# Re-ordering a retention-plus-routing kernel: when a batch's ranks, gathers, stores and transposes are issued

## The chip, the cores and the metric

The kernel runs on one core of one Trainium2 chip. The metric is device time in microseconds (us), the median of several runs. The core has a matrix engine (PE, whose weight loads the profile lists apart as PEld), a vector engine (DVE), a scalar engine (ACT), GpSimd (POOL) and a sync engine (SP). In this kernel SP issues all loads of inputs and weights, and POOL issues all stores, gathers and scatters, so each engine's instructions and DMA issues run in the order in which the program lists them.

## The reference

There are 8 batches of 576 rows with 8 heads of 64 columns, so a row is 512 wide. First comes a causal attention without softmax, whose scores decay with distance; then only the 128 rows of each batch with the highest gate score go through a two-layer MLP and are added back.

```python
scores = q @ k.T / sqrt(64)                      # per batch and head
gamma  = 1 - 2.0 ** (-5 - arange(H))
Dmat   = where(rel >= 0, gamma ** rel, 0)
x      = (scores * Dmat) @ v                     # (B, S, 512) after joining the heads
# for each batch b, capacity = 128
s      = x[b] @ w_gate
top    = argpartition(-s, capacity)[:capacity]
h      = maximum(x[b, top] @ w1, 0)              # 512 -> 1024
out[b]      = x[b]
out[b, top] = x[b, top] + sigmoid(s[top])[:, None] * (h @ w2)
```

## The kernel before

**Tiles and steps.** A batch is cut into 9 chunks of 64 rows, which makes 72 chunks in all. A step handles two neighbouring chunks (both in one 128-partition tile), so there are 36 steps (`NS`), and the loop of lines 489 to 517 runs over them, with a 37th pass that finishes the last one. A batch has an odd number of chunks, so every second batch ends in the middle of a step. `ends[b]` is the first step after batch b's last chunk has been started: 5, 9, 14, 18, 23, 27, 32, 36.

**One step.** SP loads four 256 KB pieces of a later step (q, k, v, and k again in another layout) into one of 8 `raw` buffers (lines 103 to 107). `scaled` (line 142) multiplies v by decays into `vs`, on POOL, or on ACT for the three steps that `by_act` names. `block(s)` (line 207) issues the step's matmuls on PE with 64x64 operands: the scores (`sc_ps`), the state updates (`u_ps`, copied to `st` by ACT), and, in between, the product of the step before (`crosswise(s - 1)`, into `y_ps`). `masked` (line 230, DVE) applies the causal mask and gives `am`, which the next step's `crosswise` reads. `values` (line 236, DVE) rescales `y_ps` into `xs`, the finished rows, and reduces each half with the gate weights to a score per row (`sc`). `store` (line 254, POOL) writes the rows to the output of their batch in DRAM.

**Choosing 128 rows of a batch.** When all nine chunks have scores, `total` (line 273, two small matmuls and two ACT copies) adds the two head halves, `spread` (line 288, PE and an ACT copy) lays the 576 scores out along every partition (`row`), and `compare` (line 303, DVE) counts for 128 rows at a time how many rows are ahead of each: a rank. There are five such groups, four `full` ones and one of 64 rows. Where counts are made in two parts, `joined` adds them. `one_hot` (line 318, DVE) turns ranks into a selection matrix, `rows` (line 326, PE and an ACT cast) turns that into row numbers (`idx`), and `gather` (line 337, POOL, an indirect DMA) reads those rows of the output tensor back from DRAM into `xr`. As it reads the batch's output tensor, it waits for the landing of the stores to that tensor.

**The MLP.** `turn` (line 352) transposes `xr` on PE (four transposes) and ACT copies the result to `xg`. `gates` (line 343) makes the gate. `mlp` (line 385) queues eight parts: four `up` (16 matmuls and an ACT ReLU each) and four `down` (4 matmuls each). The last `down` multiplies by the gate, adds the row and scatters the result from POOL. `some(n)` (line 389) takes n parts from that queue; `share` (lines 470 to 478) says how many a step takes.

**Order.** All of it is listed by hand. In an ordinary step the order is: loads, `run(before)`, `scaled(s + 1)`, `block(s)`, `masked(s)`, `run(mid)`, `values(s - 1)`, `store(s - 1)`, perhaps `scaled` on ACT, `run(early)`, `some(share)`, `run(late)`. `plan` puts a batch's work into one of those four slots of a step. For batches 1 to 6: total late in step `ends[b]`; spread early and three compares late in the next; the other compares and the one-hot mid, `rows` and `gather` late in `ends[b] + 2`; `turn` and `mlp` early, `gates` late in `ends[b] + 4`. Batch 0 has its own order in steps 4 and 5 (`first` and `second`, lines 413 to 440): all scores of chunks 0 to 7 are spread at once, `masked(5)` comes ahead of the last compares, and both halves of step 4's rows are stored at the end of `second`. Its `rows` and `gather` follow mid in step 6, its `turn` early in step 7.

**Loads.** `bring` (line 91) issues a load. With `few` it first waits for an earlier load so that about four are in flight; without, only the reuse of its eight semaphores limits it.

Of the kernel before, what the change touches and what calls it, by code (L numbers as in the profile page):

```python
# [9 lines left out]
F32 = mybir.dt.float32  # L10
# [25 lines left out]
def kernel(  # L36
# [66 lines left out]
    def load(s):  # L103
        x = loads.tile([P, 4, DM], F32, name="raw")
        for a in range(4):
            bring(x[:, a, :], qkvk[s, :, a * DM : (a + 1) * DM], few=s <= ends[0])
        raw[s] = x
# [31 lines left out]

    by_act = lambda s: ends[0] <= s < ends[0] + 3  # L140

# [111 lines left out]

    def store(s):
        (b, c), (b2, _) = batch(2 * s), batch(2 * s + 1)
        for i, half in enumerate(halves):
            x = xs[s][half, :].rearrange("p (c d) -> p c d", c=2)
            if b == b2:
                nc.gpsimd.dma_start(  # L259
                    out=outs[b][C * c : C * c + 2 * C, W * i : W * i + W]  # L260
                    .rearrange("(c p) d -> p c d", c=2), in_=x)
            else:
                nc.gpsimd.dma_start(out=outs[b][C * c : C * c + C, W * i : W * i + W],
                                    in_=x[:, 0, :])
                nc.gpsimd.dma_start(out=outs[b2][:C, W * i : W * i + W], in_=x[:, 1, :])

# [36 lines left out]
    def compare(b, k, j0=0, j1=S, part=0):  # L303
        if b not in rank:
            rank[b] = work.tile([P, 2, NK], F32, name="rank", bufs=2)
        n = size(k)
# [6 lines left out]

    def joined(b, n):
        nc.vector.tensor_tensor(out=rank[b][:, 0, :n], in0=rank[b][:, 0, :n],
                                in1=rank[b][:, 1, :n], op=OP.add)

# [91 lines left out]
    def go(fs):  # L409
        for f in fs:  # L410
            f()

    def first():

# [65 lines left out]
    AHEAD = 8  # L480
    bring(table, consts)
    constants()
    for s in range(AHEAD):
        load(s)
# [4 lines left out]
    for s in range(NS + 1):  # L489
# [13 lines left out]
        else:  # L503
# [4 lines left out]
            if s:  # L508
                values(s - 1)
                store(s - 1)  # L510
        if s == 2:
# [4 lines left out]
        some(share.get(s, 0))  # L516
        run(late, s)
    some(1)
    total(last, NC - 2, NC)
# [76 lines left out]
```

## Time and profile before

| | |
|---|---|
| median of 3 runs | 274.92 us (274.78 to 280.85) |
| the profiled execution | 274.87 us |
| its span in the trace | 273.2 us |
| PE busy | 231.0 us, 85% of the span |
| DVE busy | 141.7 us, 52% |
| POOL busy | 103.3 us, 38% |
| ACT busy | 58.7 us, 22% |
| moved by DMA | 56.83 MB |
| granted PE clock, mean | 0.933 |

The span is the trace's own length; the execution's time is 1.7 us longer. Busy time alone says little here: PE is the busiest engine, but the stretches in which it stands still differ along the span, so the profile is read by stage. The page's strip cuts the span into 40 slices of 6.8 us; the other views used are the waits per engine, the timeline of one engine in a stretch, and sums over stretches chosen by hand.

### The profile page before, as it was taken

How to read it: one execution, taken by the hardware profiler on the slowest of the kernel's cores; microseconds unless marked ns; L12 is line 12 of the kernel's file. 1: busy time of each engine (PE TensorE's matmuls, PEld its weight loads, DVE VectorE, ACT ScalarE, POOL GpSimd, SP SyncE). 2: the span in 40 equal slices, each digit the busy share in tenths (PEclk: the TensorE clock that was granted, in tenths of full speed). 3: DMA queues.
4: the chain of work that ended last, by engine and by line, in shares of the span. 5: the costliest groups of instructions: out<-in, count | busy, mean ns of one | idle time of the engine just before them, and what ended most of it. 6: DMA issues, size and time to landing. Idle time of an engine off the chain costs nothing.

```text
span 273.2 us, 11548 instructions
## 1 busy us (share of the span) xinstructions
PE 231.0 (85%) x5184; PEld 183.9 (67%) x5184; DVE 141.7 (52%) x354; ACT 58.7 (22%) x182; POOL 103.3 (38%) x138
## 2 busy tenths in 40 slices
PE   1845886089977999969999999699999998999992
PEld 1734785079753897649866986469868975894950
DVE  0333585243593538865864378818736487750101
ACT  1111164032210232113211231112212321121100
POOL 4264202804407353364163741824165525201101
PEclk9998568569998999999999999979999999999998
DMA  6879999999996786586577766866042113211000
GB/s 209 276 244 304 315 409 377 376 406 385 326 390 198 245 280 213 190 277 247 170 229 250 256 218 207 266 221 216 26 114 80 42 43 78 70 49 38 38 2 38
DMA packets 27601, 56.83 MB, mean 208 GB/s; under 512 B 4000, under 2 KB 4128, under 8 KB 27552
## 3 DMA queue, kind: packets, MB, share of 16 engines
q1 hardware_dynamic: 22688, 42.46, 46.6%
q0 software_dynamic: 4864, 13.64, 15.2%
q8 instruction: 41, 0.67, 1.0%
q14 instruction: 8, 0.07, 0.1%
HBM read 44.54 MB, written 11.53 MB: 205 GB/s over the span
## 4 chain that ended last, share of the span: by engine, by line
PE 60%; issue 14%; DMA 13%; DVE 8%; ACT 1%; POOLq 1%; POOL 1%; SPq 0%; DVEq 0%; ACTq 0%
PE h_ps L365 17%; PE ye_ps L373 11%; PE u_ps L165 9%; PE sc_ps L175 9%; DMA xr<-out,idx 7%; DVE scr L309 5%; DMA raw<-in_qkvk 5%; PE row_ps L296 5%; PE y_ps L196 4%; PE y_ps L186 3%; PE xg_ps L356 2%; DVE hot L322 1%; DVE am L232 1%; DMA out<-xs 1%; PE idx_ps L330 1%
## 5 line engine op out<-in xcount | busy, mean ns | idle before, releaser
L259 POOL DMA_DIRECT2D out<-xs x64 | 39.8, 625 | 90.3 <-DVE xs L241 89.9
L232 DVE TENSOR_TENSOR am<-sc_ps,table 128x512 f32<-128x512 f32 x36 | 24.9, 690 | 74.2 <-PE sc_ps L175 53.6
L365 PEld LDWEIGHTS h_ps<-xg,w_sb 128*128 128x128 f32 x512 | 59.5, 192 | 5.5 <-issue 4.4
L373 PE MATMUL ye_ps<-w_sb,hT 128*128 128x512 f32 x128 | 63.0, 624 | 0.0
L365 PE MATMUL h_ps<-xg,w_sb 128*128 128x128 f32 x512 | 62.2, 278 | 0.5 <-issue 0.4
L175 PE MATMUL sc_ps<-raw 64*64 64x64 f32 x1152 | 44.9, 231 | 11.0 <-DMA raw<-in_qkvk 5.9
L175 PEld LDWEIGHTS sc_ps<-raw 64*64 64x64 f32 x1152 | 41.0, 146 | 13.1 <-issue 7.0
L165 PE MATMUL u_ps<-vs,raw 64*64 64x64 f32 x1024 | 45.7, 232 | 3.3 <-ACT st L205 2.4
L186 PE MATMUL y_ps<-vs,am 64*64 64x64 f32 x1152 | 45.9, 232 | 3.0 <-issue 2.7
L309 DVE SCALAR_TENSOR_TENSOR scr<-row,rs,ahead 128x576 f32<-128x576 f32 (+5 forms) x47 | 42.7, 909 | 10.2 <-ACT row L301 6.1
L165 PEld LDWEIGHTS u_ps<-vs,raw 64*64 64x64 f32 x1024 | 38.1, 144 | 11.7 <-issue 6.4
L186 PEld LDWEIGHTS y_ps<-vs,am 64*64 64x64 f32 x1152 | 40.1, 144 | 3.6 <-issue 3.0
L205 ACT COPY st<-u_ps 128x256 f32<-128x256 f32 x64 | 23.7, 371 | 82.3 <-PE u_ps L165 60.9
L196 PE MATMUL y_ps<-st,raw 64*64 64x64 f32 x1024 | 39.7, 227 | 2.0 <-issue 2.0
L151 POOL TENSOR_TENSOR vs<-raw,table 128x512 f32<-128x512 f32 x33 | 34.7, 1052 | 13.3 <-DMA raw<-in_qkvk 12.8
L196 PEld LDWEIGHTS y_ps<-st,raw 64*64 64x64 f32 x1024 | 36.0, 143 | 2.1 <-issue 2.1
L373 PEld LDWEIGHTS ye_ps<-w_sb,hT 128*128 128x128 f32 x128 | 22.8, 195 | 19.5 <-issue 18.7
L250 DVE SCALAR_TENSOR_TENSOR scr<-xs,table 128x256 f32<-128x256 f32 x72 | 34.0, 473 | 2.5
L241 DVE TENSOR_TENSOR xs<-y_ps,table 128x512 f32<-128x512 f32 (+1 forms) x37 | 24.7, 667 | 3.9 <-PE y_ps L196 3.6
L367 ACT ACTIVATE hT<-h_ps 128x256 f32<-128x256 f32 x32 | 12.3, 383 | 55.7 <-PE h_ps L365 55.7
L378 DVE SCALAR_TENSOR_TENSOR o<-ye_ps,gate,xr 128x512 f32<-128x512 f32 x8 | 6.0, 751 | 30.3 <-PE ye_ps L373 17.5
L379 POOL DMA_INDIRECT out<-o,idx x8 | 9.5, 1187 | 31.1 <-DVE o L378 31.1
(35 smaller groups left out, 113.0 us busy)
## 6 DMA issues: line engine op xcount, KB each, us to landing
raw<-in_qkvk SPq DMA_DIRECT2D x144, 256.0 KB, 5.2
out<-xs POOLq DMA_DIRECT2D x64, 128.0 KB, 4.9
w_sb<-in_w SPq DMA_DIRECT2D x8, 512.0 KB, 8.9
out<-xs POOLq DMA_DIRECT2D x16, 64.0 KB, 4.9
wg<-in_w_gate SPq DMA_DIRECT2D x1, 256.0 KB
table<-in_consts SPq DMA_DIRECT2D x1, 234.5 KB
xr<-out,idx POOLq DMA_INDIRECT x8, 4.0
out<-o,idx POOLq DMA_INDIRECT x8, 4.1
```

What stands on the lines that cost most here:

```text
L151: nc.gpsimd.tensor_tensor(out=blocks(vs[s]), in0=blocks(raw[s][:, 2, :]), in1=dec[:, 0, HH * c : HH * c + H].unsqueeze(2).to_broadcast([P, ...
L165: yield lambda h=h, half=half: nc.tensor.matmul(u_ps[b][half, where(0, h)], raw[s][half, 3, where(e, h)], vs[s][half, where(e, h)], start= ...
L175: yield lambda e=e, h=h, half=half: nc.tensor.matmul(sc_ps[s][half, where(e, h)], raw[s][half, 1, where(e, h)], raw[s][half, 0, where(e, h ...
L186: yield lambda e=e, h=h, i=i, half=half: nc.tensor.matmul(y_ps[s][halves[1 - i], where(e, h)], am[s][half, where(e, h)], vs[s][half, where ...
L196: yield lambda g=g, e=e, h=h, i=i, half=half: nc.tensor.matmul(y_ps[s][halves[1 - i], where(e, h)], raw[s][half, 0, where(e, h)], st[g - 1 ...
L232: nc.vector.tensor_tensor(out=blocks(am[s]), in0=blocks(sc_ps[s]), in1=causal.unsqueeze(1).to_broadcast([P, H, C]), op=OP.mult)
L241: nc.vector.tensor_tensor(out=blocks(xs[s])[:, i0:i1, :], in0=blocks(y_ps[s])[:, i0:i1, :], in1=dec[:, 1, HH * c + i0 : HH * c + i1].unsqu ...
L250: nc.vector.scalar_tensor_tensor(scr, xs[s][:, W * e : W * e + W], 1.0, wgh, op0=OP.mult, op1=OP.mult, accum_out=sc[b][:, c : c + 1])
L259: nc.gpsimd.dma_start(out=outs[b][C * c : C * c + 2 * C, W * i : W * i + W] .rearrange("(c p) d -> p c d", c=2), in_=x)
L309: nc.vector.scalar_tensor_tensor(scr[:n, : j1 - j0], row[b][:n, j0:j1], rs[b][:n, k : k + 1], ahead[:n, at + j0 : at + j1], op0=OP.subtrac ...
L365: nc.tensor.matmul(t[:, a, :], w1_sb[:, d, P * (f + a) : P * (f + a) + P], xg[b][:, d, :], start=d == 0, stop=d == KD - 1)
L373: nc.tensor.matmul(ye[b], hT[b][:, a, :], w2_sb[:, a, :], start=a == 0, stop=a == FB - 1)
```

## The change

Six edits, all of order or of transfers:

1. `first` stores step 4's batch-0 half (the batch's last 64 rows) right after it is computed; the other half is stored in `second`.
2. Batch 0's ranks are made in three parts: columns of chunks 0 to 5 at the end of step 3, chunks 6 and 7 and then chunk 8 in steps 4 and 5. `rank` has a third slot and `joined` is called twice.
3. In `second` the compares, the one-hot, `rows` and `gather` come ahead of `masked(5)` and of the rest of the values and stores. `rows` and `gather` thus move from step 6 to step 5; the `turn` of batch 0 stays early in step 7.
4. In ordinary steps `store(s - 1)` moves to the very end of the step, behind `run(late)`, and so behind gathers and scatters on POOL.
5. For batches 1 to 6, `turn` and `mlp` move from early to late in the same step, and the parts are shared evenly from the next step on.
6. Step 5's loads are no longer `few`, its `vs` is made by POOL in place of ACT, and one small sigmoid is issued at the start.

```diff
-            bring(x[:, a, :], qkvk[s, :, a * DM : (a + 1) * DM], few=s <= ends[0])
+            bring(x[:, a, :], qkvk[s, :, a * DM : (a + 1) * DM], few=s < ends[0])
...
-    by_act = lambda s: ends[0] <= s < ends[0] + 3
+    by_act = lambda s: ends[0] < s < ends[0] + 3
...
-    def store(s):
+    def store(s, es=(0, 1)):
...
+            if 0 in es:
                 nc.gpsimd.dma_start(out=outs[b][C * c : C * c + C, W * i : W * i + W],
                                     in_=x[:, 0, :])
+            if 1 in es:
                 nc.gpsimd.dma_start(out=outs[b2][:C, W * i : W * i + W], in_=x[:, 1, :])
...
+    def part(b, k0, k1, c0, c1):
+
+        total(b, c0, c1)
+        spread(b, columns(k0, k1))
+
+    def ranked(b, k0, k1, part):
+        j0, j1 = P * k0, min(P * k1, S)
+        for k in range(k0):
+            compare(b, k, j0, j1, part)
+        for k in range(k0, k1):
+            compare(b, k, 0, j1)
...
         values(s - 1)
         store(s - 1)
-        total(0, 0, NC - 1)
-        spread(0, columns(0, full))
+        part(0, full - 1, full, 2 * full - 2, 2 * full)
         values(s, (0,))
-        total(0, NC - 1, NC)
-        spread(0, columns(full, NK))
+        store(s, (0,))
+        part(0, full, NK, 2 * full, NC)
         go(crosswise(s, (1,)))
-        for k in range(full):
-            compare(0, k, 0, P * full)
+        ranked(0, full - 1, full, 1)
 
     def second():
         s = ends[0]
         block(s, False)
+        ranked(0, full, NK, 2)
+        joined(0, full - 1)
+        joined(0, full, 2)
+        one_hot(0)
+        rows(0)
+        gather(0)
         masked(s)
-        for k in range(full):
-            compare(0, k, P * full, S, 1)
-        compare(0, full)
-        joined(0, full)
-        one_hot(0)
         values(s - 1, (1,))
-        store(s - 1)
-
-    s = ends[0] + 1
-    plan(mid, s, rows, 0)
-    plan(mid, s, gather, 0)
-    plan(early, s + 1, turn, 0)
-    plan(late, s + 1, mlp, 0)
-    plan(late, s + 1, gates, 0)
-    start = [s + 2]
+        store(s - 1, (1,))
+
+    s = ends[0]
+    plan(late, s - 2, part, 0, 0, full - 1, 0, 2 * full - 2)
+    plan(late, s - 2, ranked, 0, 0, full - 1, 0)
+    plan(early, s + 2, turn, 0)
+    plan(late, s + 2, mlp, 0)
+    plan(late, s + 2, gates, 0)
+    start = [s + 3]
...
-        plan(early, s + 4, turn, b)
-        plan(early, s + 4, mlp, b)
+        plan(late, s + 4, turn, b)
+        plan(late, s + 4, mlp, b)
         plan(late, s + 4, gates, b)
-        start.append(s + 4)
+        start.append(s + 5)
...
     share = {}
-    for i, (s0, s1) in enumerate(zip(start, start[1:])):
-        n = 0
-        for s in range(s0, s1 + 1):
-            most = 1 if s == s1 or (i and s == s0) else 2
-            more = min(most, 8 - n - (s1 - s))
-            share[s] = share.get(s, 0) + more
-            n += more
-        assert n == 8
+    for s0, s1 in zip(start, start[1:]):
+        n = s1 - s0
+        for i in range(n):
+            share[s0 + i] = -(-8 * (i + 1) // n) + (-8 * i // n)
...
     constants()
+    warm = work.tile([P, 1], F32, name="warm", bufs=1)
+    nc.scalar.activation(out=warm, in_=ones[:, :1], func=AF.Sigmoid)
...
             if s:
                 values(s - 1)
-                store(s - 1)
...
         run(late, s)
+        if s and s not in (ends[0] - 1, ends[0]):
+            store(s - 1)
```

More of the change, by code (lines that the diff above doesn't have):

```diff
@@ L261, in store @@
                     .rearrange("(c p) d -> p c d", c=2), in_=x)
-            else:
+                continue
+            if 0 in es:
                 nc.gpsimd.dma_start(out=outs[b][C * c : C * c + C, W * i : W * i + W],
                                     in_=x[:, 0, :])
+            if 1 in es:
                 nc.gpsimd.dma_start(out=outs[b2][:C, W * i : W * i + W], in_=x[:, 1, :])
@@ L304, in compare @@
         if b not in rank:
-            rank[b] = work.tile([P, 2, NK], F32, name="rank", bufs=2)
+            rank[b] = work.tile([P, 3, NK], F32, name="rank", bufs=2)
         n = size(k)
@@ L312, in compare, with joined @@
             op0=OP.subtract, op1=OP.is_gt, accum_out=rank[b][:n, part, k : k + 1])
-    def joined(b, n):
+    def joined(b, n, part=1):
         nc.vector.tensor_tensor(out=rank[b][:, 0, :n], in0=rank[b][:, 0, :n],
-                                in1=rank[b][:, 1, :n], op=OP.add)
+                                in1=rank[b][:, part, :n], op=OP.add)
     def one_hot(b):
```

## The prediction, made before the changed kernel was run

> **What bounds the kernel now.** I read the strip of 40 slices first, for where PE stands still, then PE's waits, then the timelines of the engines there, then the clock.
>
> ```profile
> PE   1845886089977999969999999699999998999992
> ...
> PEclk9998568569998999999999999979999999999998
> DMA  6879999999996786586577766866042113211000
> ```
>
> Before slice 8 (54 us) PE has holes, one of them a whole slice (7); after it PE is nearly full. So PE sets the end, and a hole taken away moves everything behind it. DMA is full from slice 4 to slice 11: loads could be late next. PE's waits:
>
> ```profile
> PE xg_ps L356 <- DMA xr<-out,idx: 12.6, 4, 7.5
> PE sc_ps L175 <- DMA raw<-in_qkvk: 5.9, 1, 5.9
> PE sc_ps L175 <- issue: 5.1, 3, 2.9
> PE idx_ps L330 <- DVE hot L322: 3.2, 4, 1.4
> ...
> PE y_ps L196 <- issue: 2.0, 1, 2.0
> ```
>
> Transposes waiting for gathers cost most: 12.6 us in four places. In PE's timeline they stand at 55.63 us (7.48, batch 0), 121.13 (2.23, batch 2), 177.84 (2.58, batch 4) and 251.52 (0.32, batch 7). Why the first is long, POOL's timeline tells:
>
> ```profile
> 30.98 0.53 POOL L263 DMA_DIRECT2D out<-xs  x1 [0.42 <-DVE xs L241]
> 42.19 0.53 POOL L265 DMA_DIRECT2D out<-xs  x1 [10.68 <-DVE xs L241]
> 42.71 0.52 POOL L263 DMA_DIRECT2D out<-xs  x1
> 43.22 0.52 POOL L265 DMA_DIRECT2D out<-xs  x1
> 48.73 1.03 POOL L339 DMA_INDIRECT xr<-out,idx  x1 [4.99 <-ACT st L205]
> ```
>
> Of batch 0's last rows one half is issued at 30.98 (L263), the other only at 42.71, because the store between them, of batch 1's rows, waits for DVE. The row numbers are ready at 42.46 (ACT's cast, 42.29 + 0.17), but the gather starts at 48.73: the L263 store of 42.71 takes 5.1 us to land, and the queue's own semaphore wait of the gather is 4.67 us. The releaser named (ACT st) isn't the one. The gather takes 6.9 us to land.
>
> **Edit by edit** (against 274.87 us, the profiled execution: 273.2 span and 1.7 around it; the median is 274.92, so the same sum serves).
>
> *Edits 1 to 3, batch 0.* Rank chain: before, row sums are spread by 34.72 us (ACT's second row copy, 34.51 + 0.21), four 512-wide compares (0.79 each) end at 36.94, `masked(5)` takes DVE to 38.38, then four 64-wide compares (0.33), one of 0.83, the join (0.17) and the one-hot (0.89) end at 41.57. After, the 384-wide compares lie at the end of step 3 (between 0.33 and 0.79 each, about 2.0 in all) where DVE sat idle for 4.0 us before 27.42. In step 4 PE's spreading shrinks from ten `row_ps` instructions in two lots (2.08 + 0.69 us) to two lots of two, 4.24 us between 30.23 and 34.47 becoming about 2.75; that gives 1.5 us. Against it the new work at the end of step 3: PE waits there for `values(2)` (DVE to 23.41), for ACT (0.3) and does six `row_ps` instructions (0.8 to 1.6 us by the clock), while before it ran on and then stood still 2.89 us, to 26.16, for nothing the profile shows. So step 4 starts late by 0 to 2 us; with the 1.5, -1.5 to +0.5. I take rows spread at 33.5 to 34.5, and then only 4 x 0.33 + 0.83 + 2 x 0.17 + 0.89 = 3.4 us to the one-hot: 37 to 38, against 41.57. `rows` and the cast add 0.6: about 38.3.
> The stores: L263's first issue, 30.98, took 6.1 us to land, so both halves land by 37 to 38.5, hardly after the row numbers. The gather is issued at 38.5 and lands 6.9 later, at 45.4.
> What is late next? PE. Its order becomes block(5), `rows`, block(6), block(7), turn. `masked(5)` is now behind the one-hot (38.0 + 0.69), and block(6)'s crosswise waits for it: block(6) starts at about 38.5, against 39.07. ACT makes vs(6) (2.02 us) behind the cast, until 40.5, just when block(6)'s last quarter needs it. From 39.07 to 48.15 PE took 9.1 us for block(6), `rows` (0.35) and block(7), 1.99 of it a hole with no releaser. So block(7) ends at 47.3 and the transposes start there, not at 55.63: **8.3 us gained**. Bounds: 10 if the hole goes too; 5 if the clock stays halved, as 85 instructions took 4.07 us at half and block(6)'s 128 took 2.9 at full.
> Loads cap this: raw(8) was issued by 38.7 us and raw(10), by 48.95, had 10.4 us to landing. In the changed kernel block(10) starts at about 58, so the supply (edit 6 starts it some 2 us earlier) just suffices.
>
> *The clock there.*
>
> ```profile
> 21.30:24.70 3.40, 1.53 (x83) 1.25 (x75) 2.04 (x6) 0.74 (x2) 1.44 (x2) 1.00 0.96 311
> 24.70:28.10 3.40, 1.94 (x53) 1.94 (x53) 0.68 (x1) 0.00 (x0) 0.79 (x2) 0.50 0.92 272
> 28.10:31.50 3.40, 2.95 (x44) 2.69 (x41) 2.42 (x9) 0.31 (x2) 1.70 (x3) 0.50 0.95 335
> ...
> 55.60:58.90 3.30, 3.27 (x88) 2.94 (x92) 0.70 (x2) 2.09 (x4) 0.00 (x0) 0.51 1.05 407
> ```
>
> The columns are the stretch, busy time of PE, PEld, DVE, ACT and POOL, then PE's granted clock. It is half from 24.7 to 38.4 and from 45.2 to 58.9. After the 7.5 us hole PE works 3.3 us at half: 1.6 us lost. Without the hole between 0 and 1.6 comes back; 0.6 taken, as the 2 us hole alone halved it at 45.2.
>
> *New waits in steps 5 to 10*: other holes without a releaser (1.79, 2.89, 1.99 before 47 us, each with one 16 KB packet of the instruction queue in the 2.3 us before PE goes on) and a load that comes late. 0 to -4; -1.0 taken, half of such a hole. The Trainium skill, "Runtime: NRT & Kernel Launch", Instruction fetch mechanics, says that crossing a 16 KB block of instructions is mostly hidden; by it this term would be 0. The trace shows holes of 1.8 to 2.9 us there.
>
> *Edit 4, gathers ahead of stores.* For batches 2 and 4 POOL issued the gather at 115.14 and 171.47 behind two stores that waited for DVE until 113.61 and 169.94; the row numbers' matmuls ended at 112.94 and 169.27. The gather gains 1.9 us. The store waits behind it instead; its rows are next read two steps later, and `scaled` stood behind both before too.
> *Edit 5.* The transposes of batch 2 come after one `down` part more (1.7 us), and step 17 takes two parts rather than one (1.7). 1.9 + 3.4 exceeds 2.23 and 2.58: both holes go, 4.8 us. At 178.30 to 181.70 the clock was 0.50 with PE busy throughout: another 1.7. Sum 6.5, bounds 3 and 6.5; **6.0** taken. The Trainium skill, "TensorE: Matmul & The Clock Gate", Part 1, ties the half clock to a whole idle window of about 3.4 us; by it a 2.58 us hole would not halve the clock and the sum would lack the 1.7. The trace has it halved.
> The new shares give step 11 two parts, not one, so the 1.38 us in which PE waited at 80.41 for batch 1's one-hot is covered: **1.4** (0 to 1.4). The 0.6 us of batches 2, 4 and 6 stay: their step keeps its one part.
> The 1.99 hole at 82.9, and 3.5 us at clock 0.51 behind it, are worth 3.7; as the instruction stream shifts, such a hole may go or come: **1.0** of 0 to 3.7.
> Tail: batch 6's transposes in step 36 are followed at once by its first `up`, which waits for ACT's copy (0.58 and hand-over): **-0.65**. Before, a `down` lay between. In steps 9 to 32 the next step's block covers that copy.
>
> *Edit 6.* The table load (1.28 us at 57.38 on ACT) moves to the start, where ACT idles until 8.85 us: nothing, as PE didn't wait behind it; 1.3 each way as bounds. vs(5) on POOL (1.05 us) lies in POOL's 3.89 us of idle before 29.38; if its load came late it would hold up the stores of step 4, 1 to 2 us.
>
> Sum: 8.3 + 0.6 - 1.0 + 6.0 + 1.4 + 1.0 - 0.65 = 15.65, so 274.87 - 15.65 = **259.2 us**. All terms at their best give 252, at their worst 272.
>
> **Rivals.**
> *A, the first stage gives half.* The clock stays halved through steps 6 and 7, or the gather waits on for stores in full DMA (loads took up to 10.5 us there). Then 8.3 becomes 5, the 0.6 goes and the 1.0 of new waits doubles: 264.5. For it: 13.7 us at half from 24.7 although PE was busy for over half of each stretch. Against: full speed came back at 38.4.
> *B, the later stages give nothing.* The transposes' holes turn into others, as PE waits for DVE's one-hots or instructions: without the 6.0, 1.4 and 1.0, 267.6. For it: DVE is 52% busy and the hot waits stay. Against: the room is 5 us for holes of 2.5. With A, 273: the change does what it says and nothing is measured.
> *C, slower: the half clock locks in.* The new order puts short PE waits (for the one-hot, for am(5), for instructions) into each 3.4 us stretch from step 3 on, and the clock never returns. Each such stretch costs 1.7 us of full-speed work; to eat 15.65 takes 9.2 of them, 31 us beyond 38.4, so it decides if PE is still at half at 70 us: then 276, and 281 at 80 us. Against: from step 8 the MLP parts fill PE (2.00 of every 2 us from 56 on).
>
> **The numbers.** The forecast case (254 to 263) gets 0.58, A 0.14, B 0.10, both 0.12, C 0.06. Within 2% (269.4 to 280.4, about what a measurement tells from no change) lies A with B and half of C, 0.15; slower 0.03, and 0.02 more for the unforeseen: faster 0.81, same 0.14, slower 0.05. The range reaches over A and B: 254 to 268.
>
> **What would show it.** The gather of batch 0 issued near 38.5 us and its transposes near 47 without a wait for `xr`; no wait for `xr` at batches 2 and 4; the one-hot wait of batch 1 gone; 0.6 us more before batch 6's first `up`; half-clock stretches shorter. Wrong if POOL's gather still starts after 44, if PE waits for `raw` in steps 8 to 11, or if holes with no releaser multiply.

## The result and the profile after

| | before | after |
|---|---|---|
| median, taken beside each other | 274.92 us | 277.8 us (276.1 to 278.88) |
| ratio, with its 95% interval | | 1.010 (1.006 to 1.014) |
| the profiled execution, and its span | 274.87, 273.2 us | 278.88, 277.2 us |
| PE busy, POOL busy | 231.0, 103.3 us | 239.8, 105.8 us |
| mean granted clock | 0.933 | 0.933 |

The forecast was 259.2 us, with a range of 254 to 268. The change brought nothing; in this comparison it is 1% slower. In two later comparisons the ratio was 0.996 and 0.984 (below). A ratio compares only those runs of each kernel that lie within 1.5% of its fastest one, as the others are in a slower state, so it is not the quotient of the two medians.

The strip of the changed kernel (40 slices of 6.9 us):

```profile
PE   0855896697998999999999998998999988999992
PEclk9985757779799999999999999999999999999997
DMA  5879999999997976788586767783313204021100
```

The empty slice around 50 us is gone, and PE is nearly full from slice 10 (69 us) on, with no slice below eight up to the last, where the kernel before had two sevens and two sixes. By this view alone the kernel should be faster. PE's waits (us in total, times, longest) tell more:

```profile
PE y_ps L186 <- issue: 7.1, 11, 2.2
PE sc_ps L175 <- DMA raw<-in_qkvk: 6.3, 1, 6.3
PE sc_ps L175 <- issue: 4.2, 7, 2.1
PE u_ps L165 <- issue: 2.8, 2, 1.8
PE idx_ps L332 <- DVE hot L324: 2.2, 4, 0.6
PE rs_ps L283 <- DVE scr L250: 2.1, 2, 1.3
...
PE y_ps L196 <- issue: 0.9, 1, 0.9
PE h_ps L367 <- ACT xg L359: 0.7, 1, 0.7
...
PE xg_ps L358 <- DMA xr<-out,idx: 0.3, 1, 0.3
```

The transposes' wait for gathered rows fell from 12.6 to 0.3 us, and the longest wait for a one-hot from 1.4 to 0.6: what the change was to remove, it removed. In its place stands "issue", time in which PE stood and the profile shows nothing that it waited for. Before, it came to 10.2 us in 7 places; now it is 15.0 us in 21. These stops are of two kinds.

**Stops in pairs.** POOL's timeline at batch 1's scatter, and then PE's beside it (start, duration, engine, line; a row with x2 stands for two matmuls):

```profile
92.35 1.26 POOL L381 DMA_INDIRECT out<-o,idx  x1 [3.55 <-DVE o L380]
93.62 1.23 POOL L259 DMA_DIRECT2D out<-xs  x2
```

```profile
92.51 0.22 PE L175 MATMUL sc_ps<-raw 64*64 64x64 f32 x2
92.52 0.22 PE L186 MATMUL y_ps<-vs,am 64*64 64x64 f32 x2
92.56 0.22 PE L175 MATMUL sc_ps<-raw 64*64 64x64 f32 x2
92.58 0.61 PE L186 MATMUL y_ps<-vs,am 64*64 64x64 f32 x2
92.95 0.32 PE L175 MATMUL sc_ps<-raw 64*64 64x64 f32 x2
93.66 0.25 PE L175 MATMUL sc_ps<-raw 64*64 64x64 f32 x1 [0.39 <-issue]
```

Up to 92.58 a pair of matmuls of each kind starts every 0.06 us. Then the starts jump to 92.95, and after four matmuls to 93.66: two stops of 0.36 and 0.60 us, 0.2 and 0.7 us after POOL began the scatter. The direct store at 93.62 causes none. The changed kernel has eleven such pairs, one beside each gather and scatter that falls into a block of 64x64 matmuls from 81 us on: gathers at 81.59, 111.39, 137.09, 169.07, 195.90 and 227.83, scatters at 92.35, 122.72, 150.05, 180.38 and 208.84. They sum to 10.4 us. Batch 0's gather, at 41.44 in a block at half clock, has none. Before, the gathers of batches 2, 4 and 6 began beside `down` parts and the scatters of batches 0 to 4 beside the last 0.4 us of an `up` part; the next block ran beside the rest of the scatter's issue, and no pair shows. Two gathers (139.85, 198.25) lay in blocks, and in that profile had no pair either.

**Stops at every 127th pair.** The other stops come singly. Counting PE's weight-load and matmul pairs from the start, each sits at 94 plus a multiple of 127 (within one): before at 221, 348, 475, 855 and 1617 (and, under 0.5 us of idle time, at 728 and 2760); after at 221 (2.15 us), 348 (0.70), 855 (2.40), 982 (2.33), 1236 (2.04), 1617 (1.17) and 4030 (1.08). 127 pairs are 254 instructions, and the profile has an instruction queue that moved 0.67 MB in 41 packets, 16 KB each; the stops end 2.2 to 2.5 us after one of those packets starts (those at 221 some 3.5 us after). In the profile after, those of 2 us and more are followed by half clock. The columns are the stretch, busy time of PE, PEld, DVE, ACT and POOL, and PE's granted clock:

```profile
45.30:48.80 3.50, 1.16 (x62) 1.02 (x62) 1.53 (x5) 2.51 (x10) 2.25 (x3) 0.99 1.05 403
48.80:52.20 3.40, 3.17 (x73) 2.72 (x73) 1.61 (x3) 0.37 (x1) 0.00 (x0) 0.50 1.05 409
52.20:55.60 3.40, 1.29 (x70) 1.15 (x73) 1.25 (x6) 1.05 (x3) 2.29 (x3) 1.00 1.05 394
55.60:59.00 3.40, 3.40 (x78) 3.28 (x71) 2.12 (x5) 0.37 (x1) 0.51 (x1) 0.50 1.05 406
...
65.90:69.30 3.40, 1.58 (x76) 1.41 (x79) 0.00 (x0) 0.90 (x4) 1.43 (x2) 0.99 1.05 350
69.30:72.70 3.40, 3.40 (x64) 3.28 (x53) 2.15 (x6) 0.43 (x2) 0.89 (x2) 0.50 1.05 390
```

Each of the stops at 46.63, 53.05 and 66.47 leaves its stretch with PE under half busy at full clock, and the next 3.4 us run at half. With PE wanted throughout, that is 1.7 us lost, and by this estimate a 2 us stop costs near 4. Not every such stretch brings half clock: in the kernel before, PE was busy for 1.61 us from 17.9 to 21.3 us, and the clock stayed full until 24.7.

**Where the time went.** I compare by the start of a step's first score matmul, at steps by which both kernels have done the same number of MLP parts:

| | before | after | gained |
|---|---|---|---|
| batch 0's transposes | 55.63 | 51.14 | 4.5 |
| step 12 (6 parts done in both) | 81.37 | 81.56 | -0.2 |
| from step 12 to batch 7's transposes | 170.15 | 173.95 | -3.8 |

The first stage gained 4.5 us and lost it again before step 12; from there on the kernel lost 3.8 where 6 were to be won.

### The profile page after: what moved, and what is told of

It is laid out like the page before. It is cut to its first block, busy times and chain, and to the rows that moved or that the text cites. A ratio compares the mean times of both kernels' runs of the same rounds, so it can differ in the third digit from the quotient of the medians.

```text
span 277.2 us, 11549 instructions
## 1 busy us (share of the span) xinstructions
PE 239.8 (87%) x5188; PEld 191.6 (69%) x5188; DVE 139.9 (50%) x361; ACT 56.6 (20%) x177; POOL 105.8 (38%) x139
## 4 chain that ended last, share of the span: by engine, by line
PE 70%; issue 13%; DVE 7%; DMA 5%; ACT 1%; POOLq 1%; POOL 1%; SPq 0%; DVEq 0%
PE h_ps L367 20%; PE ye_ps L375 15%; PE u_ps L165 9%; PE sc_ps L175 9%; DMA raw<-in_qkvk 5%; PE y_ps L196 5%; PE y_ps L186 5%; PE row_ps L298 5%; DVE scr L311 4%; PE xg_ps L358 1%; DVE am L232 1%; DVE hot L324 1%; PE rs_ps L283 1%; PE idx_ps L332 1%; DVE scr L250 1%
## 5 line engine op out<-in xcount | busy, mean ns | idle before, releaser
L175 PE MATMUL sc_ps<-raw 64*64 64x64 f32 x1152 | 52.2, 238 | 10.9 <-DMA raw<-in_qkvk 6.3
L375 PE MATMUL ye_ps<-w_sb,hT 128*128 128x512 f32 x128 | 60.0, 606 | 0.0
L186 PE MATMUL y_ps<-vs,am 64*64 64x64 f32 x1152 | 51.4, 234 | 8.0 <-issue 7.1
L175 PEld LDWEIGHTS sc_ps<-raw 64*64 64x64 f32 x1152 | 45.2, 151 | 15.6 <-issue 9.3
L165 PE MATMUL u_ps<-vs,raw 64*64 64x64 f32 x1024 | 49.0, 240 | 5.3 <-issue 2.8
L311 DVE SCALAR_TENSOR_TENSOR scr<-row,rs,ahead 128x576 f32<-128x576 f32 (+6 forms) x50 | 42.8, 856 | 15.7 <-ACT row L303 14.0
L165 PEld LDWEIGHTS u_ps<-vs,raw 64*64 64x64 f32 x1024 | 40.8, 150 | 11.8 <-issue 7.4
L186 PEld LDWEIGHTS y_ps<-vs,am 64*64 64x64 f32 x1152 | 42.5, 145 | 8.9 <-issue 8.6
L250 DVE SCALAR_TENSOR_TENSOR scr<-xs,table 128x256 f32<-128x256 f32 x72 | 31.6, 439 | 2.5
L341 POOL DMA_INDIRECT xr<-out,idx x8 | 9.0, 1130 | 60.8 <-ACT idx L335 60.8
L241 DVE TENSOR_TENSOR xs<-y_ps,table 128x512 f32<-128x512 f32 (+1 forms) x37 | 24.7, 668 | 3.8 <-PE y_ps L196 2.1
```

Source lines behind the costliest of these rows:

```text
L165: yield lambda h=h, half=half: nc.tensor.matmul(u_ps[b][half, where(0, h)], raw[s][half, 3, where(e, h)], vs[s][half, where(e, h)], start= ...
L175: yield lambda e=e, h=h, half=half: nc.tensor.matmul(sc_ps[s][half, where(e, h)], raw[s][half, 1, where(e, h)], raw[s][half, 0, where(e, h ...
L186: yield lambda e=e, h=h, i=i, half=half: nc.tensor.matmul(y_ps[s][halves[1 - i], where(e, h)], am[s][half, where(e, h)], vs[s][half, where ...
L241: nc.vector.tensor_tensor(out=blocks(xs[s])[:, i0:i1, :], in0=blocks(y_ps[s])[:, i0:i1, :], in1=dec[:, 1, HH * c + i0 : HH * c + i1].unsqu ...
L250: nc.vector.scalar_tensor_tensor(scr, xs[s][:, W * e : W * e + W], 1.0, wgh, op0=OP.mult, op1=OP.mult, accum_out=sc[b][:, c : c + 1])
L311: nc.vector.scalar_tensor_tensor(scr[:n, : j1 - j0], row[b][:n, j0:j1], rs[b][:n, k : k + 1], ahead[:n, at + j0 : at + j1], op0=OP.subtrac ...
```

## The experiments

**Which move brings the pairs.** Four variants of the changed kernel, taken together on one chip. *Edit 4 undone:*

```diff
                 values(s - 1)
+                store(s - 1)
...
-        if s and s not in (ends[0] - 1, ends[0]):
-            store(s - 1)
```

> The changed kernel with edit 4 alone undone: each store stands again right behind its values, so the gathers of batches 1 to 6 are issued behind two stores, about 1.9 us later. Theory P (PE stands about 0.36 and 0.60 us while POOL issues an indirect transfer beside a block of 64x64 matmuls): the gathers of batches 2, 4 and 6 fall beside down parts again and lose their pairs of holes, about 3 us in all; the scatters keep theirs; about 275 us. Theory I (the lost time is PE running out of instructions at every 127th pair of weight load and matmul): nothing but chance changes, 277 to 278 us.

*Edit 5 undone* (with the old `share` rule):

```diff
-        plan(late, s + 4, turn, b)
-        plan(late, s + 4, mlp, b)
+        plan(early, s + 4, turn, b)
+        plan(early, s + 4, mlp, b)
...
-        start.append(s + 5)
+        start.append(s + 4)
```

> The changed kernel with edit 5 alone undone: transposes and MLP early in their step again, old shares. Theory P: the scatters of batches 0 to 5 fall beside up parts again and lose their pairs of holes (about 1 us each, 6 in all), the 0.65 us of the tail comes back, but the 2.2 and 2.6 us waits for batch 2's and 4's gathers may return in part: about 272 to 274 us. Theory I: about 277 us, with holes at other places.

*Both undone*, the two diffs above in one kernel, which leaves edits 1 to 3 and 6:

> Edits 4 and 5 both undone: only batch 0's re-ordering, the loads and the warm-up are left. By the traces the first stage is 0.2 us behind the kernel before at step 12, with the 1.4 us one-hot wait of batch 1 back it is 1 to 2 behind; then it runs as before. Theory P: 274 to 277 us, and no paired holes beside indirect transfers. Theory I: the same time, but holes at multiples of 127 pairs where the kernel before had none.

*Scatters as plain stores*: the last `down` writes its 128 rows to the batch's first 128 rows, so the placing of chosen rows is left out:

```diff
-        nc.gpsimd.indirect_dma_start(
-            out=outs[b], out_offset=bass.IndirectOffsetOnAxis(ap=idx[b][:, :1], axis=0),
-            in_=o, in_offset=None)
+        nc.gpsimd.dma_start(out=outs[b][:P, :], in_=o)
```

> The changed kernel with the eight scatters replaced by plain stores of the same size from POOL, to the first 128 rows of each output: this leaves out the placing of the chosen rows. Everything waits for the same things. Theory P: the pairs of holes at six scatters go (about 6 us: 271 to 272 us), those at the gathers stay. Theory I, or if the holes come from the order of PE's own work: no change, 277 to 278 us.

| | us | ratio to before, 95% interval | pairs, us in sum |
|---|---|---|---|
| edit 4 undone | 274.68 | 0.986 (0.979 to 0.993) | 7 of both kinds, 6.8 |
| edit 5 undone | 272.72 | 0.982 (0.975 to 0.988) | 5 gathers, 4.6 |
| both undone | 273.62 | 0.988 (0.982 to 0.993) | 3 gathers, 2.9 |
| plain stores for scatters | 273.06 | 0.982 (0.974 to 0.990) | 6 gathers, 5.8 |

The kernel before had a median of 277.17 us beside them. In this lot the pairs follow the places. With edit 4 undone, the gathers of batches 2, 4 and 6 (111.91, 168.52, 226.78) are again beside `down` parts and have none. With edit 5 undone, the scatters begin beside `up` parts again and have none. Plain stores at the scatters' places have none, so the kind of transfer matters and not the moment alone. But the times don't follow the sums: undoing both is no better than undoing one, and with both undone three pairs stand at gathers in blocks (78.78, 134.56 and 192.96) where none was expected. With both undone the waits for gathered rows are back in the place of pairs, as the waits of this kernel show:

```profile
PE xg_ps L358 <- DMA xr<-out,idx: 3.5, 3, 2.4
```

From step 12 to batch 7's transposes this kernel takes 170.13 us, the same as before (170.15), and its whole gain of 3.4 us lies ahead of step 12.

**The changed kernel again, the gathers held, edit 1 alone, and before again.** These were taken together on another chip, where the kernel before had a median of 277.68 us. *The changed kernel, untouched:*

> The changed kernel, untouched, beside the variants on one chip. It was 1.010 of the kernel before; the variants so far were 0.982 to 0.988 of it. If the variants' gains are real and not those of a chip, this run stays at 1.00 to 1.015; if the chip made them, it comes out at 0.98 to 0.99.

*Held:* edit 4 undone, and POOL holds the scatters of batches 0 to 5 and the gathers of 1, 3 and 5 until it has issued the next step's store, which falls beside the MLP parts; batch 6's transposes come ahead of the last `down`.

```diff
-        nc.gpsimd.indirect_dma_start(
+        later(lambda: nc.gpsimd.indirect_dma_start(
             out=outs[b], out_offset=bass.IndirectOffsetOnAxis(ap=idx[b][:, :1], axis=0),
-            in_=o, in_offset=None)
+            in_=o, in_offset=None), b < last - 1)
...
+    held = []
+    def later(f, hold):
+        held.append(f)
+        if not hold:
+            flush()
+    def flush():
+        while held:
+            held.pop(0)()
...
-        plan(late, s + 2, gather, b)
-        plan(late, s + 4, turn, b)
+        plan(late, s + 2, lambda b: later(lambda: gather(b), b % 2), b)
+        plan(early if b == last - 1 else late, s + 4, turn, b)
...
+                store(s - 1)
+                flush()
...
-        if s and s not in (ends[0] - 1, ends[0]):
-            store(s - 1)
+    flush()
```

> The changed kernel with edit 4 undone, and with the scatters of batches 0 to 5 and the gathers of batches 1, 3 and 5 held back on POOL until behind the next step's store, so that they are issued beside up and down parts and not beside the 64x64 matmuls; the transposes of batch 6 go ahead of the last down part again. PE's order is otherwise the changed kernel's. Theory P: against the run with edit 4 undone (0.986 of the kernel before) eight pairs of holes of 0.95 us and 0.7 us of the tail go: 8 us less, about 0.957 of the kernel before. Theory I: only the 0.7 us, about 0.984.

*Edit 1 alone, on the kernel before:*

```diff
         values(s, (0,))
+        store(s, (0,))
...
-        store(s - 1)
+        store(s - 1, (1,))
```

> The kernel before with edit 1 alone: batch 0's last rows are stored as soon as they are there, everything else is in the old order. The gather of batch 0 then waits for its row numbers only, is issued near 42.5 us instead of 48.7 and lands near 49.4, while PE is ready at 48.2: PE's 7.5 us wait shrinks to about 1.3. If most of the first stage's gain is this edit: 0.978 to 0.985 of the kernel before. If PE, once it doesn't wait, runs into instruction holes and the halved clock instead, as in the changed kernel: 0.985 to 1.0, with holes at pairs 982 and 1236.

*The kernel before, one execution more:*

> The kernel before, for one more profile. In its first profile the gathers of batches 3 and 5 were issued beside 64x64 matmuls without a hole, which theory P alone doesn't explain: if holes of 0.95 us stand there now, it was chance; if again not, the kernel before has something that protects it.

| | us | ratio to before, 95% interval | batch 0's transposes | step 12 | step 12 to batch 7's transposes |
|---|---|---|---|---|---|
| changed | 276.79 | 0.996 (0.991 to 1.000) | 47.74 | 76.85 | 175.04 |
| held | 268.99 | 0.974 (0.966 to 0.982) | 46.06 | 76.52 | 168.64 |
| edit 1 alone | 274.33 | 0.977 (0.971 to 0.982) | 50.26 | 79.07 | 171.90 |
| before again | 275.57 | | 55.48 | 82.42 | 169.70 |

All eleven pairs are there again in the changed kernel (10.5 us in sum), and from step 12 on it is 6.4 us slower than the held version, which has the same steps and one pair left there (83.83). That version is the fastest here, though 0.957 was expected of it. Its gathers lie where this line of POOL's timeline has batch 2's, behind the store and beside a `down` part:

```profile
108.30 1.23 POOL L259 DMA_DIRECT2D out<-xs  x2 [7.30 <-DVE xs L241]
109.83 1.02 POOL L341 DMA_INDIRECT xr<-out,idx  x1 [0.30 <-PE y_ps L196]
```

Edit 1 alone brings batch 0's transposes to 50.26, 5.2 us earlier than before: most of the first stage's gain is this one store. And the kernel before, in this profile, has the pair at both of its gathers in blocks (139.15: 0.38 and 0.59 us; 197.81: 0.37 and 0.58), where the first profile of the same kernel had none. So the place isn't all. Nor does a block beside the later part of an issue make a pair: in this profile the scatter of 93.90 is followed by a block's matmuls from 94.54 on, while its issue runs to 95.14, and they show no stop.

**Where the single stops belong.** The held version once more, and three versions of it with small matmuls added at PE's start, while it waits for its first load; they shift everything behind them in PE's instruction stream and change nothing else. These ran together; the kernel before had a median of 276.67 us.

```diff
+    t = bank("shift_ps")
+    for i in range(16):   # 32 and 48 in the other two
+        nc.tensor.matmul(t[:C, :1], eye[:C, :C], eye[:C, :1], start=True, stop=True,
+                         skip_group_check=True)
     scaled(0)
```

> The held version (chosen-row reads and writes of the GpSimd queue moved so that only two of them fall beside blocks) unchanged, beside the three runs below on the same chip. Both theories: within 2 us of 269 us, or of 0.974 of the kernel before; TensorE's stops with no releaser stay at pair counts 855, 982, 1236 and 1617 in most, with single ones at other multiples of 127 beyond 94.

> The held version with 16 extra small matmul calls ahead of all others, while TensorE waits for its first load: about 32 weight-load and matmul pairs are added to the count, and nothing else. Theory: the stops left are TensorE running out of instructions at fixed counts of its own stream (every 127th pair), so they stay at counts 855, 982, 1236 or 1617, which are then other places of the program. Rival: they belong to places of the program, and move to 887, 1014, 1268, 1649. Both: time within 4 us of the held version.

> The same with 32 extra calls, about 64 pairs. Theory: stops with no releaser stay at multiples of 127 beyond 94 (855, 982, 1236, 1617). Rival: they move to 919, 1046, 1300, 1681. If the place of a stop within a stage mattered for the time, this shift by half a block of instructions would move the time most, by up to 4 us either way.

> The same with 48 extra calls, about 96 pairs. Theory: stops with no releaser stay at multiples of 127 beyond 94 (855, 982, 1236, 1617). Rival: they move to 951, 1078, 1332, 1713. Time within 4 us of the held version by both.

Stops of 0.9 us or more with no releaser, by the count of pairs at which they stand:

```
added pairs   us      ratio (95%)             counts
 0            272.83  0.988 (0.981 to 0.995)  855 982 1109 1236 1363 1490 1617 1997 4030
32            272.66  0.989 (0.978 to 1.000)  221 348 855 982 1109 1236 1363 2760
64            271.86  0.983 (0.974 to 0.993)  348 475 982 1109 1363
96            275.76  1.003 (0.997 to 1.010)  476 983 1110 1363 3395
```

No stop moved with the program: none is near 887, 919 or 951. All stay within two of 94 plus a multiple of 127, so they belong to PE's own instruction stream, and a shift puts another piece of the program there (with 32 pairs added, those at 1109 and 1236 stand ahead of `up` matmuls). Which of the multiples stand, and for how long, differs from one profile to the next even of the same kernel. One expectation failed: the held version was 1.2% faster here where 2.6% was expected. The shift by 96 is the slowest, by 2.9 us: its first stage has a stop of 4.82 us at count 476, and step 4 starts at 35.76 us where the other three have 27.3 to 29.3.

Left out of the table are two stops of 0.5 to 1.0 us that do move with the program (counts 2591 and 3885 with 32 pairs added, 2623 and 3917 with 64), each ahead of a batch's first state update, so PE can stand there for another reason that the profile doesn't name.

**The price of a pair.** To have a price that doesn't rest on reading a trace, I added gathers to the kernel before, 22 of them, one in each of steps 12 to 33, of batch 0's rows into a tile that nobody reads. The first four ran together on a new chip, where the kernel before had a median of 275.06 us.

```diff
+    def touch(s):            # called in block(s), behind the first copied(...)
+        if 12 <= s <= 33:
+            sink[s] = work.tile([P, DM], F32, name="sink", bufs=2)
+            nc.scalar.copy(out=sink[s][:, :1], in_=ones[:, :1])
+
+    def extra(s):            # called behind block(s)
+        if s in sink:
+            nc.gpsimd.indirect_dma_start(
+                out=sink[s], out_offset=None, in_=outs[0],
+                in_offset=bass.IndirectOffsetOnAxis(ap=idx[0][:, :1], axis=0))
```

> The kernel before with 22 more gathers of 128 rows (of batch 0's output, into a tile that nobody reads), one in each of steps 12 to 33, released on the GpSimd queue by a tiny ScalarE copy behind the block's first state copy, so that they run beside the block's small matmuls. Theory P (an indirect DMA's issue stops TensorE twice, about 0.95 us, beside small matmuls): 16 to 22 new pairs of stops, 14 to 21 us longer, ratio 1.05 to 1.08. Rival Q (the pairs come from something else that the changed order brought): few new pairs, under 4 us longer.

*Behind the step's stores:*

```diff
                 store(s - 1)
+                extra(s)
```

> The same 22 gathers, each placed behind the step's stores on the GpSimd queue, so that most run beside the MLP's long matmuls. Theory P: pairs only at those that still fall into blocks (about 5 of 22), 0 to 6 us longer. Rival: if any indirect DMA costs TensorE time wherever it falls, 14 to 21 us longer, as with them in blocks.

*Plain reads in the same place:*

```diff
-            nc.gpsimd.indirect_dma_start(
-                out=sink[s], out_offset=None, in_=outs[0],
-                in_offset=bass.IndirectOffsetOnAxis(ap=idx[0][:, :1], axis=0))
+            nc.gpsimd.dma_start(out=sink[s], in_=outs[0][:P])
```

> In the place of the 22 gathers in blocks, 22 plain reads of 128 rows by the GpSimd queue, of the same bytes and with the same wait. Theory P: no pairs at them, 0 to 3 us longer. Rival: if the transfer or any DMA issue of GpSimd is what stops TensorE, 14 to 21 us longer, as with the gathers.

*64 rows in place of 128:*

```diff
-                out=sink[s], out_offset=None, in_=outs[0],
-                in_offset=bass.IndirectOffsetOnAxis(ap=idx[0][:, :1], axis=0))
+                out=sink[s][:C], out_offset=None, in_=outs[0],
+                in_offset=bass.IndirectOffsetOnAxis(ap=idx[0][:C, :1], axis=0))
```

> The 22 gathers in blocks with 64 rows each in place of 128. If the pair's length goes with the number of rows, about 0.5 us each, 7 to 11 us longer; if a fixed part of the issue makes it, about 0.95 us each, as with 128 rows. Rival Q: under 4 us longer.

| | us | ratio to before, 95% interval |
|---|---|---|
| 22 gathers in blocks | 276.99 | 1.016 (0.999 to 1.032) |
| 22 gathers behind the stores | 282.77 | 1.039 (1.002 to 1.075) |
| 22 plain reads in blocks | 277.59 | 1.012 (0.977 to 1.046) |
| 22 gathers of 64 rows | 273.9 | 1.006 (1.002 to 1.010) |

The first expectation failed: 14 to 21 us more were expected, and about 4 came by the ratio (1.9 by the medians), with an interval that reaches down to nothing. But the trial was not a clean one. In its profile only 2 of the 22 lie wholly beside a block's matmuls, and PE stands for most of those two. Yet in these four profiles no gather or scatter has a pair at all, the kernel's own included (143.40 in the first and 142.68 in the last lie squarely in blocks). The second expectation (0 to 6 us more) failed too. The gathers behind the stores cost about 10 us by the ratio, as they delay the kernel's own gathers on POOL's queue: the wait for gathered rows rose to 16.2 us. So two questions were left: whether the pairs belong to single places or to a whole profile, and what their absence is worth. Two last kernels, taken together (the kernel before: 275.11 us), bear on them. *The 22 gathers released by PE early in each block*, ahead of POOL's scaling:

```diff
+            tc.add_manual_dep(          # the gather of extra(s) waits for a
+                ins.ins, begun[s],      # matmul of the third round of block(s)
+                mybir.DependencyInfo(mybir.DependencyClass.Sync, mybir.DependencyReason.DATA),
+                reason="beside a block")
...
             block(s)
+            extra(s)
+            if s + 1 < NS and 12 <= s <= 33:
+                scaled(s + 1)
```

> The kernel before with 22 more gathers of 128 rows, one in each of steps 12 to 33, each released by a matmul early in the block and ahead of the step's scaling on GpSimd, so that all run wholly beside a block. Theory: the pair comes or not for all chosen-row transfers of a profile together. If the kernel's own gathers beside blocks show it, the 22 show it too, and the time is 14 to 22 us longer; if not, 0 to 5 us longer. Rival: the pairs come and go singly, by the instructions around each one; then some 5 to 15 of the 22 have it, and the time is 5 to 14 us longer.

*The changed kernel, untouched:*

> The changed kernel once more, beside it. Theory (the pairs ate the gain of the later moves): with the pairs, 11 of them and a ratio of 0.99 to 1.02; without, a ratio of 0.95 to 0.98. Rival (something else ate it): a ratio of 0.99 to 1.02 whether the pairs are there or not.

The first came to 280.27 us, 1.019 (1.008 to 1.030), which is 5.1 us for 22 gathers and POOL's moved scaling together, 0.23 us for each gather. Thirteen of them lie wholly in a block, and none has a pair. The changed kernel came to 271.2 us, **0.984 (0.978 to 0.989)**, and none of its eleven gathers and scatters has a pair. At the same scatter as above, 4.5 us earlier in this profile, PE goes on every 0.06 us, also 0.2 and 0.7 us after the issue began, where the stops stood:

```profile
87.81 1.25 POOL L381 DMA_INDIRECT out<-o,idx  x1 [3.55 <-DVE o L380]
```

```profile
88.04 0.23 PE L165 MATMUL u_ps<-vs,raw 64*64 64x64 f32 x2
88.05 0.23 PE L186 MATMUL y_ps<-vs,am 64*64 64x64 f32 x2
88.10 0.23 PE L165 MATMUL u_ps<-vs,raw 64*64 64x64 f32 x2
88.11 0.23 PE L186 MATMUL y_ps<-vs,am 64*64 64x64 f32 x2
88.16 0.23 PE L165 MATMUL u_ps<-vs,raw 64*64 64x64 f32 x2
88.17 0.23 PE L186 MATMUL y_ps<-vs,am 64*64 64x64 f32 x2
88.22 0.22 PE L175 MATMUL sc_ps<-raw 64*64 64x64 f32 x2
88.23 0.23 PE L186 MATMUL y_ps<-vs,am 64*64 64x64 f32 x2
88.27 0.23 PE L175 MATMUL sc_ps<-raw 64*64 64x64 f32 x2
...
88.51 0.23 PE L175 MATMUL sc_ps<-raw 64*64 64x64 f32 x2
88.52 0.22 PE L186 MATMUL y_ps<-vs,am 64*64 64x64 f32 x2
88.56 0.23 PE L175 MATMUL sc_ps<-raw 64*64 64x64 f32 x2
88.58 0.28 PE L186 MATMUL y_ps<-vs,am 64*64 64x64 f32 x2
88.62 0.23 PE L175 MATMUL sc_ps<-raw 64*64 64x64 f32 x2
```

So the same program has all its pairs in two profiles and none in a third. But the later stages of the third were no faster for it. From step 12 to batch 7's transposes it took 173.61 us, against 173.95 and 175.04 with the pairs. (It is one of this kernel's longer executions here, 274.58 us.) In that stretch PE stood for single stops, and behind two of them came half clock (columns as above):

```profile
PE h_ps L367 <- issue: 2.3, 1, 2.3
PE y_ps L196 <- issue: 2.3, 2, 2.0
PE u_ps L165 <- issue: 1.9, 2, 1.2
```

```profile
93.30:96.70 3.40, 3.19 (x15) 3.19 (x16) 0.00 (x0) 0.38 (x1) 1.20 (x2) 0.50 0.95 343
188.80:192.20 3.40, 3.40 (x18) 3.40 (x18) 1.25 (x5) 0.38 (x1) 0.00 (x0) 0.51 0.02 5
```

The ratios don't give the price of the pairs either. The changed kernel's are 1.010 and 0.996 where its profile has them and 0.984 where it has none, a difference of 1.2 to 2.7 points or 3 to 7 us. But the held version, whose profiles have one pair and none, differs by 1.4 points between its two lots (0.974 and 0.988), and by 5.6 us in the same stretch (168.64 and 174.28 us). The 0.984 lies between the two expectations, outside the 0.95 to 0.98 of the theory and below the 0.99 of its rival: without the pairs the change gains 4.5 us, not 15.

So the pairs account for 10.4 us in the profile after, and moving a transfer takes its pair away in profiles that have them. That the kernel would be faster without them isn't shown, as other stops can take their place. What decides whether they come is open. Profiles taken together agree, over three lots with them (in the third by one pair in each of two profiles) and two without; the number of the chip doesn't decide it, as one number stands under lots of both kinds. Only the profiled executions can be looked into, so that the timed ones beside them behave alike is assumed.

## Why the prediction was wrong

It forecast 15.65 us. In the profiled execution 10.15 of the miss lie after step 12 and 9.5 before it (the sum's terms up to there are 8.3 + 0.6 - 1.0 + 1.4 = 9.3, and -0.2 was measured).

**Edits 1 to 3, 8.3 (bounds 5 to 10): mis-sized, and partly given back.** The profile gives 4.5, the other two of the changed kernel 5.7 and 7.9. The step that failed is "step 4 starts late by 0 to 2 us". Its block started 6.5 us later (29.18 against 22.65), and even against 26.16, where PE went on after its stop in the kernel before, 3.0 later. Each new item had been named, and together they were undersized: 1.26 + 0.81 us of waiting for `values(2)`, 0.41 for ACT and 1.65 for the six spreading matmuls at half clock make 4.1; a stop at 14.06 lasted 1.0 longer; and half clock set in at 18.1, not at 24.7. POOL's timeline has the consequence:

```profile
33.08 1.24 POOL L259 DMA_DIRECT2D out<-xs  x2 [2.58 <-DVE xs L241]
34.34 1.05 POOL L264 DMA_DIRECT2D out<-xs  x2
41.44 1.04 POOL L341 DMA_INDIRECT xr<-out,idx  x1 [6.05 <-ACT idx L335]
```

The gather was issued at 41.44, not near 38.5, and now it did wait for the row numbers (ACT's `idx`) and not for a store: edit 1 worked as told. The rest followed as forecast: no wait for `xr` at the transposes, which stood at the end of PE's own queue, 3.8 us later than forecast.

**New waits in steps 5 to 10, -1.0 (0 to -4): mis-sized.** Stops at 53.05 (2.33 us) and 66.47 (2.04) are new, 4.4 us, and the half clock behind each costs another 1.7. Less the 1.6 us of half clock and the 1.4 us of one-hot wait that the kernel before had there, that is 4.8 us by this estimate, and it is where the 4.5 us went between batch 0's transposes and step 12. I had counted the stops of the kernel before and allowed half of one; they stand at multiples of 127 pairs of PE's stream, and which of these places become stops differs from one execution to the next. The Trainium skill, "Runtime: NRT & Kernel Launch", Instruction fetch mechanics, calls the crossing of a 16 KB line mostly hidden, since the sequencer issues more slowly than the lines are filled. Most of the 41 crossings agree with it; in the seven that the profile after shows, the stop was 0.7 to 2.4 us.

**The clock, +0.6: didn't come.** Half clock ended at 72.7 us, not at 58.9.

**Edits 4 and 5, 6.0 (3 to 6.5): the failed step.** The waits of batches 2 and 4 are gone (2.23 + 2.58), and so is the half clock at 178.3. The step that failed is that nothing would come in their place. The issue of the moved transfers was costed at nothing: "The store waits behind it instead" for edit 4, and "the next step's block covers that copy" for edit 5. Nothing was said of what PE runs while POOL issues a gather. Edit 4 moved the gathers of batches 2, 4 and 6 from beside a `down` part into a block, edit 5 the scatters from the end of an `up` part into a block. Eight of the eleven pairs stand at these moved transfers, the other three at the gathers of batches 1, 3 and 5; all eleven take 10.4 us in this execution. Of single stops behind step 12 the sum had only the one at 82.9, as a gain; in the profile without pairs such stops and the half clock behind them kept the later stages as long (173.61 us). So these stages gave little or nothing of the 6.0 in either case: the kernel as a whole gained 4.5 us in the runs beside that profile, and 3.8 to 5.6 us are there by step 12 (77.60 and 76.85 against 81.37 and 82.42). What the runs show in the place of the 6.0 is stops without a releaser; which kind comes, and why, stays open.

**The small terms.** Batch 1's one-hot wait (1.4) is gone as forecast. The stop at 82.9 (1.0 taken) fell from 2.21 to 1.17, without half clock behind it. The tail's -0.65 is there as 0.7 us (`h_ps` waiting for `xg`). Edit 6 cost nothing that the profile shows.

**Rivals.** A and B together (273) named most of what happened. The first stage gave about half (4.5 of 8.3), with the clock at half beyond 58.9 us, and the waits of the later stages turned into others; B even had "as PE waits for DVE's one-hots or instructions". The pairs beside POOL's transfers are in neither. (A's own terms, 3.3 + 0.6 + 1.0, give 264.1, not 264.5.) C's number is the nearest: 276 if PE is still at half at 70 us, and from 69.3 to 72.7 it is. But the clock didn't lock, as C has it: it was full in four stretches between 31.7 and 69.3 us, and from 72.7 us on. Of the signs named for a wrong forecast, "holes with no releaser multiply" is the one that showed; a wait for `raw` in steps 8 to 11 did not. The forecast gave 0.12 to A and B together and 0.06 to C, and treated such stops as a matter of the first 90 us.

## What to carry to other kernels

An instruction moved on one engine's queue is also moved against what the other engines run at that time: look at what the matrix engine will execute beside each moved issue. A gather or scatter beside long matmuls had no stop here, one beside a run of small ones had two in some profiles; what that costs a whole kernel these runs don't settle. A wait that is removed gives its time only if the stretch behind it can take it up; where the matrix engine runs hundreds of small matmuls, its own instruction stream can be the next limit, and a gain of 5 us can be given back to two stops before the next stage. Such stops differ between executions of one program, so profile a kernel more than once before pricing them. Keep the one edit that carries most of the gain (here one early store) apart from the moves around it, and time them singly.

## What the runs showed of the hardware

- Beside 64x64 matmuls, an indirect DMA issued by POOL can stop PE twice, 0.36 and 0.60 us. Profiles that were taken together have it at nearly all such places or at none (11, 11 and 0 in the same kernel). No stop showed where the block began only 0.6 us after the issue. Where no pair showed, 22 more gathers and a moved scaling cost 5.1 us together.
- PE's single stops stand at fixed counts of its instruction stream, 127 weight-load and matmul pairs apart, and stay there when the program is shifted by 32, 64 or 96 pairs; each lasts 0.3 to 4.8 us, and which of them occur differs between executions. Most end 2.2 to 2.5 us after a 16 KB packet of the instruction queue starts.
- A stretch of 3.4 us in which PE was busy for 1.2 to 1.6 us was followed by 3.4 us at half clock, in three cases of the profile after. In the profile before, 1.61 us in such a stretch (from 17.9 us) was followed by full clock.
